# First products of W_o's gradient between the last sums of the recurrence's backward pass, and LayerNorm loads behind three chunks of rows

## The chip, the core and the metric

The kernel runs on one core of one Trainium2 chip. Its time is the device time of one execution in microseconds (us); the median of several executions counts. Five engines run beside each other: TensorE (PE) multiplies, VectorE (DVE) and ScalarE (ACT) empty accumulators and do elementwise work, GpSimd (POOL) copies and issues DMAs, SyncE (SP) issues DMAs. Each runs its own instructions in order and waits on semaphores for the others.

## What is computed

One transformer layer, forward and backward: the output and the gradients of all eleven inputs that have one. A recurrent attention block with 32 heads of 128 goes through 64 segments of 32 tokens, with 8 memory rows handed from segment to segment; a gated MLP follows; both stand behind a LayerNorm that is scaled and shifted by rows made from `c` and `w_mod`. What bears on the change:

```python
for s in range(n_seg):                                   # 64 segments, in order
    h = jnp.concatenate([mem, xs], axis=1)               # 8 memory rows + 32 tokens = 40 rows
    q, k, v = (einsum('btd,dhe->bhte', h, W) for W in (Wq, Wk, Wv))
    ...
    o = jnp.einsum('bhqk,bhke->bhqe', p, v)
    o = jnp.einsum('bhte,hed->btd', o, Wo)
    mem = o[:, :M, :]
_out, _vjp = jax.vjp(_f, A_x, A_mem0, A_Wq, A_Wk, A_Wv, A_Wo, B_w_gate, B_w_up, B_w_down, c, w_mod)
```

W_o's gradient is, for each head, the product of two row matrices over all 64 x 40 rows: the attention output before W_o, and the gradient after W_o. The gradients of Wq, Wk and Wv are such products too.

## The kernel before

The program is one long list of instructions in phases; the two at whose border the change lies are `phase4` and `phase5`. A scheduler puts the instructions of each engine in order by what it holds to be ready, unless `pin` forbids it: `pin(i0, engines)` chains all instructions traced since `i0` on each engine in the order of the program text, and `pin_behind` puts all of a stretch behind one instruction.

**Phase 4, the recurrence backward.** A loop over the 64 segments, last one first, pinned on all engines. Each segment ends in a 512-column sum `dh_ps` of 64 narrow products, a second sum of the query part (`dhq_ps`, folded to `dh_ft`), and a row store to `DHA`, whose second half (turn by TensorE, copy by VectorE, store by GpSimd) is put off in a list `later` and taken out by `pop_later`. The 8 last rows of each segment (the *tail*) are gathered for four segments at a time; class `TailRows` multiplies them by the three weights in 96 narrow products `dh_tps` in seven pieces (16, 24, 8, 8, 16, 8, 16), one piece per call of `chunk`. `split` then writes the sum as two bf16 halves, hi by ScalarE and lo by VectorE (L312, L313), into tile `dS`; 8 products fold them (`dh_b_ft`, L323), VectorE casts (L331), TensorE turns (`dh_b_tp`, L335), VectorE copies (L337), and GpSimd stores to `DHB` (L341). The tail of group 1 (segments 4 to 7) is worked off within the last segments. That of group 0 is collected in the last segment, so `finish` (L2225 on) runs all of it behind the loop: split of group 1, all seven pieces of group 0, split of group 0, then everything in `later`. Its sum lives in the single bank of pool `psb`, which group 1's sum holds until its split. The loop's other accumulators are six banks of pool `psp`, tag `p`.

**Phase 5, weight gradients and the first LayerNorm backward.** 36 chunks: nine for W_o, then nine each for Wq, Wk, Wv. A chunk has up to four heads, its rows are loaded into `rows5` (three buffers; 20 positions x up to 512 columns on 128 partitions), and each head of a W_o chunk is one bank `gps5o` with 20 products of 512 columns (L2121). Pool `psG` has four banks. `load_rows(i + 2)` is issued at chunk `i`; the first three chunks' rows go on SP's queue alone, by `rows_in` (L1931), later ones half on ScalarE's. Chunk 0 is prepared during the last segment: `p5_first` loads the gradient rows (`dyrows`, L1918) and 12 of chunk 0's 20 positions (`rows_a`) into the place of `WoT`, which is free by then, and `p5_second` (L1939) the gradient's memory rows. So 48 of chunk 0's 80 products read only these (the profile writes `WoT`); the other 32 wait for the rest of the chunk's rows. SP's loads are pinned among themselves from `load_rows(0)` to the loads of chunk 5; LayerNorm's are not in that chain.

The LayerNorm part goes through 16 tiles of 128 rows (`ln_tile`): loads of `x0`, of the gradient rows `dhb` in eight pieces from `DHA` and `DHB` (L362, L363) and of `dx1` (L1981), VectorE statistics (L1990), two products into a sum (`acc_ps`, L1999 and L2002), and a store. `ln_load(0)` stands at chunk 5 in the text, and `ca1_bc` (L369) is loaded at the top of the phase.

Of the kernel before, what the change touches and what calls it, by code (L numbers as in the profile page):

```python
# [7 lines left out]
BF16 = mybir.dt.bfloat16  # L8
F32 = mybir.dt.float32
# [3 lines left out]
PSUM = bass.MemoryType.PSUM  # L13
# [27 lines left out]
class K:  # L41
# [1502 lines left out]
    def phase4(self):  # L1544
        nc, tc, cfg, io = self.nc, self.tc, self.cfg, self.io
        D, DC, H, E, L, M, T, G, NS = cfg.D, cfg.DC, cfg.H, cfg.E, cfg.L, cfg.M, cfg.T, cfg.G, cfg.NS
# [5 lines left out]
        with self.p4_ctx as ctx:  # L1552
# [3 lines left out]
            pt = ctx.enter_context(tc.tile_pool(name="p4pt", bufs=1, reuse_waits="tile"))  # L1556
            rxp = ctx.enter_context(tc.tile_pool(name="p4rx", bufs=3, reuse_waits="tile"))
            sb2 = ctx.enter_context(tc.tile_pool(name="p4s2", bufs=2, reuse_waits="tile"))
            psp = ctx.enter_context(tc.tile_pool(name="p4ps", bufs=6, space=PSUM, reuse_waits="tile"))
            psb = ctx.enter_context(tc.tile_pool(name="p4psb", bufs=1, space=PSUM, reuse_waits="tile"))  # L1560
            NP = 3
            PG = 4
# [133 lines left out]
            i0 = len(self.traced())  # L1696
# [14 lines left out]
            i0 = len(self.traced())  # L1711
            for s in reversed(range(NS)):
# [175 lines left out]
                g = s // 4  # L1888
# [10 lines left out]
                then = None  # L1899
                if s == 0:  # L1900
                    def then(rb):
                        nc.sync.dma_start(io["out_2"].rearrange("o m (c x) -> (o m c) x", c=DC), rb[0:M * DC, :])

                self.store_rows(psp, sb2, ft, self.DHA[s], "dh", "p", then)
                if s4 == 0:
                    tail.begin(s, [WvT, WkT, WqT])
            store_rows_x(0)
            self.pin(i0)
            tail.finish()

    def p5_first(self):

# [8 lines left out]
    def rows_in(self, dst, dram, hl, g0, ng, a, b, o, qs):  # L1921
# [3 lines left out]
        for k, runs in enumerate((((0, Q, 32 * hl), (Q, Q + T2, 32 * hl + M)),  # L1925
                                  ((0, Q, 32 * hl + Q), (Q, c, 32 * hl + M + T2), (c, Q + T2, 96 + 8 * hl)))):
            to = dst.rearrange("(s k) t x -> k s t x", k=2)[k]
            for t0, t1, r in runs:
                lo, hi = max(a, t0), min(b, t1)
                if lo < hi:  # L1930
                    qs[k].dma_start(to[:, lo - o:hi - o, 0:ng * E],  # L1931
                                    dram[:, r + lo - t0:r + hi - t0, g0:g0 + ng, :].rearrange("s t g e -> s t (g e)"))

    def p5_second(self):

        nc, cfg, M, NS = self.nc, self.cfg, self.cfg.M, self.cfg.NS
        Q = M // 2
        for k in range(2):
            nc.sync.dma_start(self.dyrows[:, 0:Q, :].rearrange("(s k) t d -> k s t d", k=2)[k],  # L1939
                              self.DHA[1:NS + 1, Q * k:Q * k + Q, :])  # L1940

    def phase5(self):
# [7 lines left out]
        assert KR <= 128  # L1950
        with ExitStack() as ctx:
            ctx.enter_context(self.wo_ctx)
            rp = ctx.enter_context(tc.tile_pool(name="p5g_r", bufs=1, side="right", reuse_waits="tile"))
            hrows = rp.tile([128, NTP, D], BF16, name="hrows")
            lp = ctx.enter_context(tc.tile_pool(name="p5g_l", bufs=3, reuse_waits="tile"))
# [2 lines left out]
            sb1 = ctx.enter_context(tc.tile_pool(name="p5a_s1", bufs=1, reuse_waits="tile"))  # L1958
            sb2 = ctx.enter_context(tc.tile_pool(name="p5a_s2", bufs=2, reuse_waits="tile"))
            psAcc = ctx.enter_context(tc.tile_pool(name="p5a_psAcc", bufs=1, space=PSUM, reuse_waits="tile"))  # L1960
            ca1_bc = self.mod_bc(wp, 1, "ca1_bc", plus_one=True)
            sel = wp.tile([128, 2, 128], BF16, name="sel5")
            nc.vector.memset(sel[:], 0.0)
            for i in range(2):
# [87 lines left out]
            if not getattr(cfg, "skip_wgrad", False):  # L2052
                Q, T2, A = M // 2, T // 2, self.p5_ahead
                op_ = ctx.enter_context(tc.tile_pool(name="p5g_o", bufs=3, reuse_waits="tile"))
                psG = ctx.enter_context(tc.tile_pool(name="p5g_ps", bufs=4, space=PSUM, reuse_waits="tile"))
                kk = [0]

                def next_eng():
                    kk[0] += 1
                    return "act" if kk[0] % 2 == 0 else "dve"  # L2060

                def load_h(k):
                    if k == 0:
                        nc.sync.dma_start(hrows[:, Q:NTP, :], self.H1ROWS[:, :].rearrange("(p t) d -> p t d", t=T2))
                        return
                    for i in range(2):
                        nc.sync.dma_start(hrows[:, 0:Q, :].rearrange("(s k) t d -> k s t d", k=2)[i],
                                          self.AOA[0:NS, Q * i:Q * i + Q, :])

                chunks = [(hl, g0, min(4, (H - hl + 2) // 3 - g0)) for hl in range(3) for g0 in (0, 4, 8)]  # L2070
                todo = [(x, kind, outw, ch) for (x, kind, outw) in ((self.OSR, "o", io["out_6"]), (self.DQR, "qkv", io["out_3"]),
                                                                  (self.DKR, "qkv", io["out_4"]), (self.DVR, "qkv", io["out_5"]))
                        for ch in chunks]
                loaded = {}

                def load_rows(i):
                    if i >= len(todo) or i in loaded:
                        return
                    x, _, _, (hl, g0, ng) = todo[i]
                    t = loaded[i] = lp.tile([128, NTP, 4 * E], BF16, name="rows5")  # L2080
                    self.rows_in(t[:, :, :], x, hl, g0, ng, 0, NTP - A if i == 0 else NTP, 0,
                                 (nc.sync, nc.sync if i < 3 else nc.scalar))

                i0 = len(self.traced())
                load_rows(0)
                load_rows(1)
                load_rows(2)
                n_ln = len(todo) - 6
                for i, (_, kind, outw, (hl, g0, ng)) in enumerate(todo):
                    load_rows(i + 2)  # L2090
                    if 4 <= i <= 5:
                        load_h(i - 4)
                    if i == 5:
                        self.pin(i0, [mybir.EngineType.SP])
                    rows = loaded.pop(i)
                    if i == 5:
                        ln_load(0)
                    while ln_done[0] * (n_ln - 5) < (i - 5) * NT and ln_done[0] < NT:
                        ln_step()
                    if i >= n_ln:  # L2100
                        mod_grads(i - n_ln)
                    h0 = 3 * g0 + hl
                    if kind == "qkv":
                        for c in range(DC):
                            ps = psG.tile([128, 4 * E], F32, name="gps5", tag="g")
                            for tp_ in range(NTP):
                                nc.tensor.matmul(ps[:, 0:ng * E], lhsT=hrows[:, tp_, c * 128:(c + 1) * 128],  # L2107
                                                 rhs=rows[:, tp_, 0:ng * E], start=(tp_ == 0), stop=(tp_ == NTP - 1))
                            ot = op_.tile([128, 4 * E], BF16, name="ot5")
                            self.evac(next_eng(), ot[:, 0:ng * E], ps[:, 0:ng * E])  # L2110
                            nc.gpsimd.dma_start(outw[c * 128:(c + 1) * 128, h0:h0 + 3 * (ng - 1) + 1:3, :],  # L2111
                                                ot[:, 0:ng * E].rearrange("p (h e) -> p h e", e=E))
                    else:
                        pss = [psG.tile([128, D], F32, name="gps5o", tag="g") for _ in range(ng)]
                        order = list(range(NTP - A, NTP)) + list(range(Q, NTP - A)) + list(range(Q))
                        parts = (order[0:6], order[6:A], order[A:NTP - Q], order[NTP - Q:]) if i == 0 else (order,)
                        for part in parts:
                            for gg in range(ng):
                                for tp_ in part:
                                    src = (self.rows_a, tp_ - NTP + A) if i == 0 and tp_ >= NTP - A else (rows, tp_)  # L2120
                                    nc.tensor.matmul(pss[gg][:], lhsT=src[0][:, src[1], gg * E:(gg + 1) * E], rhs=dyrows[:, tp_, :],  # L2121
                                                     start=(tp_ == order[0]), stop=(tp_ == order[-1]))
                        for gg, ps in enumerate(pss):
                            ot = op_.tile([128, D], BF16, name="ot5o")
                            self.evac(next_eng(), ot[:], ps[:])
                            nc.gpsimd.dma_start(outw[h0 + 3 * gg], ot[:])
    def run_pipeline(self, n, stages, deepest_first=False, after=lambda it: None):
        ns = len(stages)
        states = {}
        for it in range(n + ns - 1):  # L2130
            for k in (reversed(range(ns)) if deepest_first else range(ns)):
                j = it - k
                if 0 <= j < n:
                    states[j] = stages[0](j) if k == 0 else stages[k](j, states[j])
                    if k == ns - 1:
                        states.pop(j, None)
            after(it)
# [26 lines left out]
class TailRows:  # L2164
# [57 lines left out]
        self.k.later.append(summed)  # L2222
        return True

    def finish(self):  # L2225
        self.split()
        while self.pieces:
            self.chunk()
        self.split()
        while self.k.later:  # L2230
            self.k.pop_later()

# [84 lines left out]
```

## Time and profile before

| what | value |
|---|---|
| median of 3 runs | 3039.75 us (3037.28 to 3044.77) |
| the profiled execution's own time | 3037.14 us |
| its span, first to last instruction | 3035.4 us |
| TensorE busy, mean granted clock | 2958.5 us (97%), 0.995 |
| last product of the loop's last segment starts | 2458.33 us |
| first product of chunk 0 (data of the last segment's loads) | 2468.22 us |
| first product of chunk 0 that needs rows loaded in phase 5 | 2479.81 us |
| first product of chunk 1 | 2487.53 us |
| first and last LayerNorm products (`acc_ps`) | 2565.3 us, 2926.3 us |

All moments are microseconds from the span's start. A line of the timeline gives start, duration, engine, source line, operation and tile, a count of like instructions merged, and in brackets the idle time of the engine before it with what ended it. `PE` durations include the way through the array; like products start closer together than they last. `SPq` is SP as an issuer of DMAs. `WoT<-DAROWS` and `WoT<-OSR` are the early loads for chunk 0, `rows<-OSR` those of phase 5.

### The profile page before, as it was taken

To read this page: it belongs to the slowest core of one execution; us is meant where nothing else is said; L and a number is where in the kernel's file an instruction comes from. 1 tells how busy PE (TensorE), PEld (TensorE's weight loads), DVE (VectorE), ACT (ScalarE), POOL (GpSimd) and SP (SyncE) were. 2 spreads that over 40 slices of the span, in tenths; PEclk is the share of its full clock that TensorE was granted. 3 is DMA by queue.
4 is the path that set the end of the run, shared out by engine and by line. 5 is a ranking of instruction groups with operands and counts; after the bars stand their busy time and mean duration, and the time that the engine had idled before them with its cause. 6 is when DMAs were issued, how large, how long until landed. Compare 5 with 4: busy or idle time off the path is not lost.

```text
span 3035.4 us, 106027 instructions
## 1 busy us (share of the span) xinstructions
PE 2958.5 (97%) x43975; PEld 1852.1 (61%) x44049; DVE 1605.5 (53%) x3746; ACT 1290.0 (42%) x3185; POOL 1219.8 (40%) x2642
## 2 busy tenths in 40 slices
PE   6999999999998999999999999999999999999999
PEld 3666666666665544446577777777777754445454
DVE  5566656656655788723455555555555532222221
ACT  2555555555554533312355555555555521101111
POOL 2555555555545222211244444444444422333322
PEclk9999999999999999999999999999999999999999
DMA  9888888888889899988699999999999997666574
GB/s 305 220 223 204 212 224 213 208 218 214 212 210 275 208 229 227 246 258 262 188 245 249 248 245 247 248 248 246 246 248 247 246 287 258 224 194 217 175 242 148
DMA packets 837350, 703.15 MB, mean 232 GB/s; under 512 B 537634, under 2 KB 709826, under 8 KB 835972
## 3 DMA queue, kind: packets, MB, share of 16 engines
q1 hardware_dynamic: 709764, 484.85, 63.9%
q0 software_dynamic: 54512, 148.63, 15.5%
q10 hardware_dynamic: 72592, 62.89, 6.7%
q8 instruction: 346, 5.67, 0.8%
q14 instruction: 136, 1.11, 0.1%
HBM read 295.09 MB, written 276.35 MB: 188 GB/s over the span
## 4 chain that ended last, share of the span: by engine, by line
PE 89%; DMA 4%; issue 3%; DVE 2%; ACT 1%; POOL 1%; SPq 0%; another core or an unknown queue 0%; DVEq 0%; POOLq 0%; ACTq 0%
PE pass_ps L255 14%; PE gps L2107 11%; PE dh_ps L215 8%; PE g_ps L1768 6%; PE pass_ps L658 5%; PE gps5o L2121 4%; PE dhq_ps L223 4%; PE at_ps L223 4%; PE gps L1444 3%; PE mm L1286 3%; PE dh_tps L215 3%; PE turn_ps L828 2%; PE dp_ps L1745 2%; PE tps L1676 2%; PE mm L1261 1%
## 5 line engine op out<-in xcount | busy, mean ns | idle before, releaser
L2107 PE MATMUL gps<-rows,hrows 128*128 128x512 bf16 (+2 forms) x2124 | 415.6, 355 | 1.9
L2107 PEld LDWEIGHTS <-hrows 128*128 128x128 bf16 x2160 | 211.2, 98 | 204.6
L61 ACT ACTIVATE ot<-gps 128x512 bf16<-128x512 f32 (+3 forms) x75 | 41.3, 551 | 371.8 <-PE gps L2107 211.6
L1813 POOL COPY dOst<-RAd 96x512 bf16<-96x512 bf16 x128 | 75.5, 614 | 302.2 <-DVE RAd L63 302.2
L63 DVE CAST ot<-gps 128x512 bf16<-128x512 f32 (+3 forms) x76 | 48.2, 634 | 273.9 <-PE gps L2107 186.8
L658 PE MATMUL pass_ps<-Wv,hT 128*32 128x512 bf16 (+2 forms) x2304 | 188.2, 357 | 0.0
L2111 POOL DMA_DIRECT2D out_dram<-ot x108 | 81.6, 755 | 260.6 <-DVE ot L63 135.8
L255 PEld LDWEIGHTS <-hT 128*32 128x32 bf16 x4096 | 125.1, 97 | 95.3 <-DMA Wq<-in_A_Wq_dram 5.9
L1034 POOL TENSOR_TENSOR Pst<-Pst,rden 120x1408 bf16<-120x1408 bf16 x63 | 159.9, 2538 | 50.7 <-issue 27.2
L61 ACT ACTIVATE dVT<-g_ps 128x480 bf16<-128x480 f32 (+1 forms) x192 | 104.6, 545 | 95.6 <-PE g_ps L1768 95.1
L63 DVE CAST Vst<-pass_ps 96x512 bf16<-96x512 f32 x128 | 87.3, 682 | 106.5 <-ACT RBv L61 99.8
L215 PE MATMUL dh_ps<-WvT,dVT 128*32 128x512 bf16 x2048 | 134.5, 383 | 0.2
L255 PE MATMUL pass_ps<-Wq,hT 128*32 128x512 bf16 x2048 | 125.6, 383 | 5.8 <-DMA Wq<-in_A_Wq_dram 5.8
L2121 PE MATMUL gps5o<-WoT,rows 128*128 128x512 bf16 x580 | 127.8, 379 | 2.4 <-DMA rows<-OSR 1.7
L223 PE MATMUL at_ps<-Wo,OT 128*32 128x256 bf16 x4096 | 124.6, 274 | 3.0 <-DMA Wo<-in_A_Wo_dram 2.6
L658 PE MATMUL pass_ps<-Wv,hb 128*32 128x512 bf16 (+2 forms) x636 | 127.3, 346 | 0.0
L255 PE MATMUL pass_ps<-Wk,hT 128*32 128x512 bf16 x2048 | 124.1, 379 | 1.8 <-POOL hT L547 1.1
L793 POOL DMA_DIRECT2D Vst<-RBv x192 | 99.6, 524 | 59.7 <-ACT ET L840 38.2
L255 PE MATMUL pass_ps<-WoT,dyT 128*32 128x256 bf16 (+1 forms) x3072 | 122.4, 308 | 0.9 <-ACT dyT L1887 0.9
L223 PE MATMUL dhq_ps<-WqT,dQT 128*32 128x256 bf16 x4096 | 122.9, 273 | 0.0
L215 PE MATMUL dh_ps<-WkT,dKT 128*32 128x512 bf16 x2048 | 122.3, 380 | 0.0
L223 PEld LDWEIGHTS <-dQT 128*32 128x32 bf16 x4096 | 109.6, 97 | 15.9
(457 smaller groups left out, 6976.1 us busy)
## 6 DMA issues: line engine op xcount, KB each, us to landing
OSR<-Ost SPq DMA_DIRECT2D x64, 352.0 KB
OT<-OT SPq DMA_DIRECT2D x64, 352.0 KB
VT<-VTr SPq DMA_DIRECT2D x64, 352.0 KB
PS<-Pst SPq DMA_DIRECT2D x64, 352.0 KB
OT_l<-OT SPq DMA_DIRECT2D x64, 352.0 KB
Pst_l<-PS SPq DMA_DIRECT2D x64, 352.0 KB
VT_l<-VT SPq DMA_DIRECT2D x64, 352.0 KB
DVR<-rows_x POOLq DMA_DIRECT2D x64, 352.0 KB, 5.9
```

The costliest lines, as they stand in the source:

```text
L61: return nc.scalar.activation(out, in_, AF.Copy)
L63: return nc.vector.tensor_copy(out, in_)
L215: self.nc.tensor.matmul(ps[32 * j:32 * j + 32, :], lhsT=lhsT, rhs=w, start=(n < 4), stop=(n >= total - 4), tile_position=(0, 32 * j))
L223: nc.tensor.matmul(ps[32 * j:32 * j + 32, :], lhsT=x[k], rhs=w[k][:, 256 * d:256 * d + 256], start=(n == 0), stop=(n == total - 1), tile_p ...
L255: self.nc.tensor.matmul(ps[32 * j:32 * j + 32, :], lhsT=lhs(c), rhs=rhs, start=(c == 0), stop=(c == DC - 1), tile_position=(0, 32 * j))
L658: nc.tensor.matmul(ps[32 * j:32 * j + 32, o * E:(o + n) * E], lhsT=lhsT, rhs=wc[:, 3 * a + hl:3 * (a + n - 1) + hl + 1:3, :], start=(c == ...
L793: nc.gpsimd.dma_start(Vst[96 + 8 * j:104 + 8 * j, :], rb[32 * j + o:32 * j + o + 8, :])
L1034: nc.gpsimd.tensor_tensor(Pst[0:120, :, :], Pst[0:120, :, :], rden[:, :].unsqueeze(2).to_broadcast([120, G, 128]), op=ALU.mult)
L1286: nc.tensor.matmul(hp[:], lhsT=xT[:, fc, :], rhs=wT[:, fc, :], start=(n == 0), stop=(n == 2 * FC - 1))
L1768: nc.tensor.matmul(ps[:, j, 0:w], lhsT=lh[:, g * GW:(g + 1) * GW], rhs=rh[:, g * GW:g * GW + w], start=True, stop=True)
L2107: nc.tensor.matmul(ps[:, 0:ng * E], lhsT=hrows[:, tp_, c * 128:(c + 1) * 128], rhs=rows[:, tp_, 0:ng * E], start=(tp_ == 0), stop=(tp_ == ...
L2121: nc.tensor.matmul(pss[gg][:], lhsT=src[0][:, src[1], gg * E:(gg + 1) * E], rhs=dyrows[:, tp_, :], start=(tp_ == order[0]), stop=(tp_ == o ...
```

## The change

- `psp`, the six banks of the recurrence, stays open into phase 5 and takes the place of `psG`. The tail's last sum (`dh_tps` of group 0) takes a bank of `psp` instead of the one of `psb`.
- `finish` takes one entry out of `later` behind each piece of the tail. Behind the last piece the split goes to a tile of `rxp` instead of `dS`; then three groups of 16 products of chunk 0 (positions 0 to 3, 4 to 7 and 8 to 11 of its order, four heads each) are issued, with one entry of `later` taken out behind each.
- TensorE's order in `finish` is pinned, behind the loop.
- In phase 5, `ca1_bc` and `ln_load(0)` are issued at chunk 1, in SP's chain behind the rows of chunks 0, 1 and 2; every later DMA of SP is put behind the chain's end.
- The store of `out_2` goes from SP's queue to GpSimd's.

```diff
@@ phase4
+            self.ps_ctx = ExitStack()
+            psp = self.psp = self.ps_ctx.enter_context(tc.tile_pool(name="p4ps", bufs=6, space=PSUM, reuse_waits="tile"))
...
                     def then(rb):
-                        nc.sync.dma_start(io["out_2"].rearrange("o m (c x) -> (o m c) x", c=DC), rb[0:M * DC, :])
+                        nc.gpsimd.dma_start(io["out_2"].rearrange("o m (c x) -> (o m c) x", c=DC), rb[0:M * DC, :])
...
             store_rows_x(0)
-            self.pin(i0)
-            tail.finish()
+            last, i0 = self.pin(i0), len(self.traced())
+            tail.psb, tail.ptag = psp, "p"
+            tail.finish([lambda k=k: self.p5_products(range(4 * k, 4 * k + 4)) for k in range(3)],
+                        rxp.tile([128, G, 128], BF16, name="rows_x")[:].rearrange("p g x -> p (g x)"))
+            self.pin(i0, [mybir.EngineType.PE])
+            self.pin_behind(i0, last, [mybir.EngineType.PE])
...
+    def p5_chunk0(self):
+
+        D, NTP, Q, A = self.cfg.D, self.cfg.L // 2, self.cfg.M // 2, self.p5_ahead
+        self.p5_order = list(range(NTP - A, NTP)) + list(range(Q, NTP - A)) + list(range(Q))
+        self.p5_ps = [self.psp.tile([128, D], F32, name="gps5o", tag="p") for _ in range(4)]
+
+    def p5_products(self, ks, rows=None):
+
+        if ks[0] == 0:
+            self.p5_chunk0()
+        E, NTP, A, order = self.cfg.E, self.cfg.L // 2, self.p5_ahead, self.p5_order
+        for gg, ps in enumerate(self.p5_ps):
+            for k in ks:
+                t = order[k]
+                src = (rows, t) if t < NTP - A else (self.rows_a, t - NTP + A)
+                self.nc.tensor.matmul(ps[:], lhsT=src[0][:, src[1], gg * E:(gg + 1) * E], rhs=self.dyrows[:, t, :],
+                                      start=(k == 0), stop=(k == NTP - 1))
@@ phase5
-            ca1_bc = self.mod_bc(wp, 1, "ca1_bc", plus_one=True)
+            ca1_bc = wp.tile([128, D], F32, name="ca1_bc")
...
-                psG = ctx.enter_context(tc.tile_pool(name="p5g_ps", bufs=4, space=PSUM, reuse_waits="tile"))
...
                 for i, (_, kind, outw, (hl, g0, ng)) in enumerate(todo):
+                    if i == 1:
+                        self.mod_bc(wp, 1, "ca1_bc", plus_one=True, t=ca1_bc)
+                        ln_load(0)
                     load_rows(i + 2)
                     if 4 <= i <= 5:
                         load_h(i - 4)
-                    if i == 5:
-                        self.pin(i0, [mybir.EngineType.SP])
                     rows = loaded.pop(i)
                     if i == 5:
-                        ln_load(0)
+                        last, i1 = self.pin(i0, [mybir.EngineType.SP]), len(self.traced())
...
+                        if i == 0:
+                            pss = self.p5_ps
+                            self.p5_products(range(A, NTP - Q), rows)
+                            self.p5_products(range(NTP - Q, NTP), rows)
...
+                self.pin_behind(i1, last, [mybir.EngineType.SP])
@@ TailRows
-    def finish(self):
+    def finish(self, between=(), home=None):
         self.split()
         while self.pieces:
             self.chunk()
+            if between:
+                self.k.pop_later()
+        if between:
+            self.home = home
         self.split()
+        for f in between:
+            f()
+            self.k.pop_later()
         while self.k.later:
             self.k.pop_later()
```

More of the change, by code (lines that the diff above doesn't have):

```diff
@@ L1558, in phase4 @@
             sb2 = ctx.enter_context(tc.tile_pool(name="p4s2", bufs=2, reuse_waits="tile"))
-            psp = ctx.enter_context(tc.tile_pool(name="p4ps", bufs=6, space=PSUM, reuse_waits="tile"))
+            self.ps_ctx = ExitStack()
+            psp = self.psp = self.ps_ctx.enter_context(tc.tile_pool(name="p4ps", bufs=6, space=PSUM, reuse_waits="tile"))
             psb = ctx.enter_context(tc.tile_pool(name="p4psb", bufs=1, space=PSUM, reuse_waits="tile"))
@@ L1952, in phase5 @@
             ctx.enter_context(self.wo_ctx)
+            ctx.enter_context(self.ps_ctx)
+            psG = self.psp
             rp = ctx.enter_context(tc.tile_pool(name="p5g_r", bufs=1, side="right", reuse_waits="tile"))
@@ L2104, in phase5 @@
                         for c in range(DC):
-                            ps = psG.tile([128, 4 * E], F32, name="gps5", tag="g")
+                            ps = psG.tile([128, 4 * E], F32, name="gps5", tag="p")
                             for tp_ in range(NTP):
@@ L2113, in phase5 @@
                     else:
[L2114 to L2117, printed above, removed]
+                        if i == 0:
+                            pss = self.p5_ps
+                            self.p5_products(range(A, NTP - Q), rows)
+                            self.p5_products(range(NTP - Q, NTP), rows)
+                        else:
+                            pss = [psG.tile([128, D], F32, name="gps5o", tag="p") for _ in range(ng)]
                             for gg in range(ng):
[L2119 to L2122, printed above, removed]
+                                for n, t in enumerate(self.p5_order):
+                                    nc.tensor.matmul(pss[gg][:], lhsT=rows[:, t, gg * E:(gg + 1) * E], rhs=dyrows[:, t, :],
+                                                     start=(n == 0), stop=(n == NTP - 1))
                         for gg, ps in enumerate(pss):
```

## The prediction

> **What bounds the kernel.** I read the page first (busy time, then the chain that ended last):
>
> ```profile
> PE 2958.5 (97%) x43975; PEld 1852.1 (61%) x44049; DVE 1605.5 (53%) x3746; ACT 1290.0 (42%) x3185; POOL 1219.8 (40%) x2642
> PE 89%; DMA 4%; issue 3%; DVE 2%; ACT 1%; POOL 1%; SPq 0%; another core or an unknown queue 0%; DVEq 0%; POOLq 0%; ACTq 0%
> ```
>
> TensorE is the bound: a change gains only by closing holes between its products. Next come TensorE's waits. From 2490 us to the end the view is empty. In the stretch 2458 to 2490 us, which the change rebuilds, it says (total, times, longest):
>
> ```profile
> PE gps5o L2121 <- DMA rows<-OSR: 1.7, 2, 1.1
> PE dh_b_ft L323 <- ACT dS L312: 0.7, 1, 0.7
> PE dh_b_tp L335 <- DVE dh_b_rb L337: 0.5, 1, 0.5
> PE dh_tp L335 <- DVE dh_tb L331: 0.5, 1, 0.5
> PE dh_b_tp L335 <- DVE dh_b_tb L331: 0.4, 1, 0.4
> PE dh_tps L215 <- DVE dh_rb L337: 0.4, 1, 0.4
> PE dh_b_ft L323 <- DVE dS L313: 0.4, 1, 0.4
> ```
>
> Eight holes. TensorE's timeline places them and gives the pace of the products:
>
> ```profile
> 2458.33 0.27 PE L240 MATMUL dh_ft<-foldsel,dh_lo 128*128 128x32 bf16 x4
> 2459.76 1.91 PE L215 MATMUL dh_tps<-WvT,dh_tail 128*32 128x512 bf16 x32 [0.40 <-DVE dh_rb L337]
> 2461.49 1.91 PE L215 MATMUL dh_tps<-WkT,dh_tail 128*32 128x512 bf16 x32
> ...
> 2468.22 10.52 PE L2121 MATMUL gps5o<-WoT 128*128 128x512 bf16 x47
> 2479.81 7.07 PE L2121 MATMUL gps5o<-WoT,rows 128*128 128x512 bf16 x31 [1.07 <-DMA rows<-OSR]
> 2487.53 12.70 PE L2121 MATMUL gps5o<-WoT,rows 128*128 128x512 bf16 x57 [0.66 <-DMA rows<-OSR]
> ```
>
> Last SP's own timeline: between the last segment's transposes and the rows of chunk 0 stand LayerNorm's loads, and one of them waits for the tail's store:
>
> ```profile
> 2461.01 2.90 SPq L1776 DMA_TRANSPOSE rows_x<-dQT  x1
> 2464.01 0.53 SPq L1902 DMA_DIRECT2D out_dram<-dh_rb  x1
> ...
> 2472.47 0.26 SPq L363 DMA_DIRECT2D dhb<-DHB  x1
> 2472.83 0.34 SPq L369 DMA_DIRECT2D ca_bc<-MODROW  x1
> 2473.23 33.02 SPq L1931 DMA_DIRECT2D rows<-OSR  x18
> ```
>
> **The sum.** From 2458.33 to the first product of chunk 1 at 2487.53 TensorE does a fixed lot of work, the same before and after. By start-to-start pace: 32 tail products take 1.73 us (2459.76 to 2461.49), 0.054 each, so 96 take 5.19. A chunk product takes 0.219 (49 in 10.74 us in the chain), so 80 take 17.54. Two folds of 8 (0.30 each in the chain) 0.60, three turns of 0.06 0.18, the four products at the start 0.15. Together 23.66 us of 29.20. The difference, 5.5 us, is what the holes cost; their idle columns add up to 4.71 (0.54, 0.40, 0.70, 0.36, 0.44, 0.54, 1.07, 0.66), because each stop also loses the overlap of a product's way through the array (it lasts 0.379 and starts every 0.219).
>
> **Tail and folds, part by part.** (1) The first piece no longer needs the bank that group 1 holds until its split ends at 2459.62; it can start at 2458.48, and the turn `dh_tp`, whose cast ends at 2459.08, comes behind 16 products (0.87 us): both first stops go. (2) The fold of group 1 then comes behind 24 more products, at 2460.7; its halves are there since 2459.62. (3) Its turn needs the cast, about 0.5 us from fold to turn (2458.60 to 2459.13 in the last segment), and only 8 products (0.43) cover that. A stop of 0.1 to 0.3 is new; I take 0.2. (4) 48 products more bring 2464.2. The split of group 0 (0.60 and 0.69 us, L312 and L313) lies beside 16 chunk products (3.5 us), the cast (0.44) beside the next 16, the copy and store beside the last 16. (5) Accumulators: chunk 0 holds four of six banks, the tail's sum one until about 2465.8. If the third head is given that one, it wants it at 2466.0, so 0 to 0.3; I take 0, for other banks are long empty.
>
> **Early data.** The products now start at 2464.2, not 2468.2. What they read was issued from 2445.82 to 2451.5 (3.5 MB); 2450 to 2460 ran at 403 and 379 GB/s, and the transposes behind on the same queue show from 2461 on. So it lies there by about 2463. Price 0 to 4.0 us (the old start proves only 2468.2); I take 0.
>
> **Rows.** SP is free at 2464.0 and goes straight to chunk 0's rows, 9.2 us earlier. The 48 products end at 2475.1, the next 16 need rows. Before, the first rows were there 6.6 us after the first issue (2473.23 to 2479.81) and chunk 1's 14.3 us after it (2487.49). Now the transposes fill the DMA engines until 2466 (100% in 2464 to 2466), and the stores of `DKR` and `DQR` (0.35 MB each) come in between, 2 us at 340 GB/s, while `ca1_bc` (0.26 MB, 0.8 us) stands behind. Chunk 0: 2464.0 + 6.6 + 2 to 3 = 2472.6 to 2473.6, before 2475.1. Chunk 1: 2464.0 + 14.3 + 1.2 to 3.2 = 2479.5 to 2481.5; wanted at 2482.2. Margin 0.7 us and more: chunk 0's two stops go, the second only just. Chunk 2 waits for the `DQR` store (issued 2468.07, such stores land in 3.0 to 5.0 us) and is wanted at 2499.7; its 2 MB take 6 us.
>
> The Trainium skill ("DMA: Bandwidth & Descriptors", Anatomy of one DMA) gives a DMA about 2.0 us plus its bytes at 436 GB/s. By it the 3.93 MB before would have taken 11.0 us; the trace shows 14.3, so the trace's value is used. By the rule the margin of chunk 1 would be over 3 us and its rival below would lose most of its chance.
>
> **Moved without price.** The `out_2` store: 0.53 us off SP, 0.54 us onto GpSimd, which then idles 4.9 us to 2465.51. LayerNorm tile 0 loads some 12 us later (SP reaches it at about 2476), and GpSimd's store of group 0's `DHB` row goes from 2468.6 to about 2472.3, landing 3.9 us on; behind these loads on SP stands only chunk 3, whose buffer is free at 2482 and wanted at 2513. Tile 0's first product is at 2565.3. Tile 1 loads behind chunk 5's loads, at about 2550, for products at 2578 (2583.1 before): 28 us of cover, and if it were gone each us would stall TensorE. Six banks instead of four only relax the evacuations. VectorE (53% busy) and ScalarE (42%) have room.
>
> Sum: 5.5 - 0.2 = 5.3 us. The profiled execution, 3037.14 us (1.74 around its span of 3035.4), becomes 3031.8. The median of the runs shown is 2.6 above that execution, and the forecast goes by the median: 3039.75 - 5.3 = **3034.4**. A measurement of this kernel can tell some 0.3%, 9.1 us, from no change: no hole that could bring that is in this stretch.
>
> **Rivals.**
> *Chunk 1's rows come late.* SP's issue of them meets the stores or waits for earlier loads (SP waits for its own `rows` loads at 2486 to 2500 before). By 1 to 3 us: 3035.5 to 3037.5. For it: the thin margin. 15%.
> *It does not do what it says for the rows*: a buffer of chunks 0 or 1 lies over tiles still read, and SP's first issue stays near 2472. The two DMA stops, shifted, take back most: chunk 1 at 2472 + 14.3 = 2486.3, gain 1.2, 3038.5. Against it: the transposes read these tiles until 2467.6 at most. 9%.
> *Slower: VectorE waits for LayerNorm.* Only TensorE is pinned in the tail. Before, VectorE took `x0`'s statistics at 2468.67, right behind the tail's copies. If the scheduler sets them ahead of group 0's cast, TensorE's turn, now pinned in front of the last 16 early products at 2471.7, waits for `x0`. That load now stands behind 5.6 MB of rows; with stores about 6.6 MB from 2466 on, at 335 GB/s, and 1.8 us to report (before, chunk 0's bytes had moved by 2478 and TensorE went on at 2479.81): 2487.5; statistics 0.69 and cast 0.44 make 2488.7. A hole of 17 us. It also costs clock:
>
> ```profile
> 1495.28 0.56 PE L1768 MATMUL g_ps<-Pst_l,dOst 128*128 128x120 bf16 x4 [5.40 <-DMA dOst<-RBd]
> 1496.00:1498.00 2.00, 2.00 (x23) 2.00 (x21) 0.00 (x0) 0.75 (x2) 0.83 (x5) 0.50 0.01 4
> ```
>
> Behind a hole of 5.40 us the granted clock (third from the right) is 0.50, and 1.00 again from 1502: some 2.7 us lost. Net 17.0 + 2.7 - 5.3 = 14.4 slower, 3054. It decides as soon as the cast is over 2472. For it: VectorE's operations were drawn ahead already (`dc_t` at 2463.45). Against it: by any reckoning `x0` is ready long after the cast's input. 9%.
>
> The Trainium skill ("TensorE: Matmul & The Clock Gate", Part 1: The HAM clock gate) has the clock halved after about 3.4 us of idleness; a hole of 3.30 us at 1316.6 already left 0.55 behind it here. No hole of the forecast is near either.
>
> **How the numbers follow.** Forecast 61%, late rows 15%, rows as before 9%, VectorE 9%, other (a lucky median, an order better than I see) 6%. The own range of the forecast is 3031 to 3037 (the runs before spread over 7.5 us, the early data up to 4). With both middle rivals, their spread and the low end: 3029.5 to 3042; the VectorE case and half of the last are left out. Faster by over 0.3%: 7%, a median below 3030.6; slower by over 0.3%: 10%; within: 83%.
>
> **What would show it.** TensorE's waits from 2458 to 2485: one of about 0.2 at `dh_b_tp`, none for `rows<-OSR`, none for `dS`; first chunk product near 2464.2, chunk 1 near 2482.2; SP's first `rows<-OSR` near 2464. A wait of chunk 1's first product shows rival one, a late first issue rival two, a hole at the second `dh_b_tp` rival three. Any wait of TensorE behind 2500, at `acc_ps` above all, would show LayerNorm's loads too late, which this sum holds for covered.

## The result, and the profile after

The changed kernel takes 3033.84 us in the median of 22 runs (3029.84 to 3047.09) against 3039.78 for the kernel before in 22 runs beside it; the ratio is 0.9984, 95% interval 0.9976 to 0.9992, so 2.4 to 7.3 us less. The forecast was 3034.4, 5.3 less.

The page's first lines of the changed kernel. TensorE's share has risen by one point. It also leads the chain that ended last as before, with 86% (89% before), and "issue" has 5% there (3%); that shift was not taken apart.

```profile
span 3033.1 us, 106112 instructions
PE 2963.8 (98%) x44049; PEld 1853.1 (61%) x44049; DVE 1605.2 (53%) x3746; ACT 1288.1 (42%) x3185; POOL 1215.5 (40%) x2643
```

TensorE's timeline of the rebuilt stretch in the changed kernel (start, duration, what, count; a bracket would show idle time):

```profile
2461.21 0.27 PE L240 MATMUL dh_ft<-foldsel,dh_lo 128*128 128x32 bf16 x4
2461.41 1.05 PE L215 MATMUL dh_tps<-WvT,dh_tail 128*32 128x512 bf16 x16
...
2464.26 0.61 PE L215 MATMUL dh_tps<-WkT,dh_tail 128*32 128x512 bf16 x8
2464.87 0.23 PE L335 MATMUL dh_b_tp<-ident,dh_b_tb 128*128 128x128 bf16 x1
...
2467.73 3.63 PE L1954 MATMUL gps5o<-WoT 128*128 128x512 bf16 x16
2471.20 0.36 PE L323 MATMUL dh_b_ft<-foldsel,rows_x 128*128 128x32 bf16 x8
...
2478.36 7.07 PE L1954 MATMUL gps5o<-WoT,rows 128*128 128x512 bf16 x32
2485.27 15.06 PE L2147 MATMUL gps5o<-WoT,rows 128*128 128x512 bf16 x69
```

No line has a bracket, and the view of TensorE's waits is empty from 2458 us to the end: all eight stops are gone. From the second `dh_ft` products to chunk 1's first product, **the stretch** from here on, it is 2485.27 - 2461.21 = 24.06 us, against 29.20 before: 5.14 us less. This execution came to the stretch 2.88 us later than the one before (2461.21 against 2458.33), in work that the change does not touch. So the spans differ by 2.3 us only (5.14 - 2.88), and single executions are compared by the stretch.

SP's timeline of the changed kernel:

```profile
2464.32 2.87 SPq L1777 DMA_TRANSPOSE rows_x<-dQT  x1
2467.30 19.28 SPq L1936 DMA_DIRECT2D rows<-OSR  x14
2486.62 0.70 SPq L369 DMA_DIRECT2D ca_bc<-MODROW  x1
2495.36 0.34 SPq L2002 DMA_DIRECT2D x<-in_A_x_dram  x1
```

The rows do follow the transposes at once. But their 14 loads take 19 us to issue, and SP's waits say why: the first load of chunk 1, the fifth in all, is held until 2475.85, until a store of `DQR` has landed.

```profile
SPq L1936 <- DMA DQR<-rows_x: 5.3, 1, 5.3
```

### The profile page after: what moved, and what is told of

Read it like the earlier page. It is cut to its first block, busy times and chain, and to the rows that moved or that the text cites. A ratio compares the mean times of both kernels' runs of the same rounds, so it can differ in the third digit from the quotient of the medians.

```text
span 3033.1 us, 106112 instructions
## 1 busy us (share of the span) xinstructions
PE 2963.8 (98%) x44049; PEld 1853.1 (61%) x44049; DVE 1605.2 (53%) x3746; ACT 1288.1 (42%) x3185; POOL 1215.5 (40%) x2643
## 4 chain that ended last, share of the span: by engine, by line
PE 86%; issue 5%; DMA 4%; DVE 2%; POOL 1%; ACT 1%; SPq 0%; ACTq 0%; POOLq 0%; DVEq 0%
PE pass_ps L255 14%; PE gps L2132 9%; PE dh_ps L215 8%; PE g_ps L1769 6%; PE pass_ps L658 5%; PE gps5o L2147 4%; PE dhq_ps L223 4%; PE at_ps L223 4%; PE gps L1444 3%; PE mm L1286 3%; PE dh_tps L215 3%; PE turn_ps L828 2%; PE dp_ps L1746 2%; PE tps L1677 2%; PE mm L1261 1%
## 5 line engine op out<-in xcount | busy, mean ns | idle before, releaser
L2147 PE MATMUL gps5o<-WoT,rows 128*128 128x512 bf16 x560 | 121.4, 379 | 0.0
```

The costliest lines, as they stand in the source:

```text
L2147: nc.tensor.matmul(pss[gg][:], lhsT=rows[:, t, gg * E:(gg + 1) * E], rhs=dyrows[:, t, :], start=(n == 0), stop=(n == NTP - 1))
```

## The experiments

The theory: the change is worth the sum of its stops, those for rows through the loads' part and those of the tail through the rest, and the two need each other. The rivals are in the texts on record. Every kernel is read by its stretch, from one profiled execution each; where several runs were timed, the ratio to the kernel before stands beside it. The two kernels that were profiled twice agree with themselves within 0.2 us.

| kernel | stretch, us | expected by the theory |
|---|---|---|
| before; once more | 29.20; 29.36 | 29.2 or about 30.7 |
| changed; once more | 24.06; 24.05 | 24.0 to 24.6 |
| loads_only | 28.85 (27.2 at full clock) | 27.2 |
| products_only | 33.35 | 32 to 33 |
| tail_old_bank | 25.29 | 25.3 |
| products_behind | 26.23 | 26.2 to 26.4 |
| hrows_early | 30.60 | 26.7 to 27.7 |
| four_buffers | 25.19 | 24.0 to 24.2 |
| small_loads_first | 25.19 | 24.0 to 24.2 |
| ln_behind_two | 24.05 | 24.0 to 24.2 |
| second_late | 24.05 | 24.0 to 24.1 |
| second_late_small | 24.18 | 24.0 to 24.1 (A), 24.1 to 25.2 (B) |

**The loads' part alone (loads_only).**

```diff
+                    if i == 1:
+                        self.mod_bc(wp, 1, "ca1_bc", plus_one=True, t=ca1_bc)
+                        ln_load(0)
                     load_rows(i + 2)
...
+                self.pin_behind(i1, last, [mybir.EngineType.SP])
```

> The kernel before with the loads' part alone: ca1_bc and LayerNorm tile 0 behind the rows of three chunks, later SP loads behind that chain; tail, products and banks as before. Read in the stretch from the last segment's second dh_ft products to chunk 1's first product (29.20 us before, 24.06 with the whole change). My theory: SP issues the first rows right behind the transposes, some 9 us earlier, so TensorE's two stops for rows (1.07 and 0.66, and 0.16 of lost overlap each) go and the six stops of the tail stay: stretch 27.2, time 2.0 us less. Rival (the rows were late for their buffers, not for LayerNorm): stretch 29.2, time the same.

Measured: ratio 0.9995 (0.9984 to 1.0005), not told from no change. Both stops for rows are gone and the tail's six are left, as expected, but from the first of the 48 early products to the next one behind them it takes 12.05 us (2470.93 to 2482.98). In the kernel before, at the pace of 0.216 us of these products, it would be 10.36 (the 10.52 of its line hold the last product's way through the array too):

```profile
2470.93 12.21 PE L2122 MATMUL gps5o<-WoT 128*128 128x512 bf16 x47
```

The table by stretches (each engine's busy time, then TensorE's granted clock, third from the right) shows the reason:

```profile
2472.00:2474.00 2.00, 2.00 (x6) 0.76 (x5) 0.00 (x0) 0.00 (x0) 1.09 (x3) 0.50 1.05 345
2474.00:2476.00 2.00, 2.00 (x8) 0.79 (x7) 0.00 (x0) 0.00 (x0) 0.00 (x0) 0.76 0.56 218
```

The clock fell to half behind the tail, which cost 1.7 us; from 2476 on it is 1.00 again. With 32 products behind 2482.98 chunk 1 starts near 2489.9, so the stretch is 28.85, and 27.2 without the clock's loss: the loads' part would be worth 2.0 us at full clock. This is a corrected figure of one execution; the runs' ratio does not show it.

**All but the loads' part (products_only).** In the changed kernel:

```diff
-            ca1_bc = wp.tile([128, D], F32, name="ca1_bc")
+            ca1_bc = self.mod_bc(wp, 1, "ca1_bc", plus_one=True)
...
-                    if i == 1:
-                        self.mod_bc(wp, 1, "ca1_bc", plus_one=True, t=ca1_bc)
-                        ln_load(0)
...
+                    if i == 5:
+                        self.pin(i0, [mybir.EngineType.SP])
                     rows = loaded.pop(i)
                     if i == 5:
-                        last, i1 = self.pin(i0, [mybir.EngineType.SP]), len(self.traced())
+                        ln_load(0)
...
-                self.pin_behind(i1, last, [mybir.EngineType.SP])
```

> The whole change without its loads' part: tail, products between the sums and shared banks as changed, ca1_bc and LayerNorm's loads as before. My theory: the rows still stand behind LayerNorm's loads on SP, and these wait for group 0's DHB store, which the interleaving makes about 3.7 us later; so the first rows go out near 2477 on before's clock, TensorE runs dry behind its 48 early products for some 8 us, and chunk 1 starts 3 to 4 us later than before: stretch 32 to 33, slower by 3 to 4 us. Rival (the tail's six stops carry the gain by themselves): stretch 25.5 to 26, faster by 3.5 us. Between them: the scheduler sends the rows ahead of the waiting load, stretch 29, no change.

Measured: ratio 1.0014 (1.0005 to 1.0023), slower; stretch 33.35, 4.15 more than before. TensorE's timeline, SP's, and the clock behind the stop:

```profile
2470.00 3.62 PE L1954 MATMUL gps5o<-WoT 128*128 128x512 bf16 x15
2480.50 9.31 PE L1954 MATMUL gps5o<-WoT,rows 128*128 128x512 bf16 x32 [6.89 <-DMA rows<-OSR]
2489.64 15.70 PE L2146 MATMUL gps5o<-WoT,rows 128*128 128x512 bf16 x70
```

```profile
2470.51 0.43 SPq L2048 DMA_DIRECT2D wmod<-in_w_mod_dram  x1
2471.04 0.37 SPq L369 DMA_DIRECT2D ca_bc<-MODROW  x1
2471.46 36.89 SPq L1936 DMA_DIRECT2D rows<-OSR  x18
```

```profile
2482.00:2484.00 2.00, 2.00 (x6) 0.72 (x5) 0.00 (x0) 0.00 (x0) 0.00 (x0) 0.50 1.11 349
```

The tail's stops are gone, and the time they held comes back as one stop of 6.89 us for rows, behind which the clock is halved. The 4.15 us add up: the first rows are used 24.21 us behind the `dh_ft` products instead of 21.48 (2.73 more), 32 products take 9.14 us instead of 6.91 (2.23 more), and the stop of before at chunk 1, 0.8 from start to start, is gone. The size was as expected; the wait that I had named was not. In the kernel before SP does wait for a store to `DHB`:

```profile
SPq L363 <- DMA DHB<-dh_b_rb: 2.3, 1, 2.3
```

Here it does not: four loads of `DHB` run through from 2467.60, the other four are set behind the rows at 2508. The first rows go out 15.17 us behind the `dh_ft` products, as before (14.90); a `w_mod` load of 0.77 MB that now stands just ahead of them would take 2.3 us at 340 GB/s and fits the rest, which was not tried by itself.

**The tail's bank (tail_old_bank) and the products' place (products_behind).**

```diff
-            tail.psb, tail.ptag = psp, "p"
```

> The whole change, but group 0's tail sum in the old single bank, which group 1's sum holds until its split has ended. My theory: the first piece waits for VectorE's lo half as before, 1.2 to 1.3 us, and nothing gives that back: stretch 25.3. Rival (chunk 1's rows come only just in time in the changed kernel, so TensorE's lead there is worth nothing): stretch 24.1 to 24.4.

```diff
         self.split()
+        while self.k.later:
+            self.k.pop_later()
         for f in between:
             f()
-            self.k.pop_later()
-        while self.k.later:
-            self.k.pop_later()
```

> The whole change, but chunk 0's 48 early products behind the last fold and turn instead of between them. My theory: split (0.60 and 0.69), fold, cast (0.44) and turn of group 0 stand bare again: TensorE stops about 2.2 us, stretch 26.2 to 26.4. Rival (these stops are hidden in the wait for rows anyway): stretch 24.1 to 24.5.

Measured: 25.29 (1.23 lost) and 26.23 (2.17 lost). Stops come back at the same places of the work. In tail_old_bank it is one at the tail's first piece, in place of the two of before around it, and VectorE's lo half ends it; in products_behind there are three at group 0's folds and turn:

```profile
2469.71 1.05 PE L215 MATMUL dh_tps<-WvT,dh_tail 128*32 128x512 bf16 x16 [1.17 <-DVE dS L313]
```

```profile
2467.82 0.27 PE L323 MATMUL dh_b_ft<-foldsel,rows_x 128*128 128x32 bf16 x4 [0.75 <-ACT rows_x L312]
2468.55 0.27 PE L323 MATMUL dh_b_ft<-foldsel,rows_x 128*128 128x32 bf16 x4 [0.46 <-DVE rows_x L313]
2469.35 0.23 PE L335 MATMUL dh_b_tp<-ident,dh_b_tb 128*128 128x128 bf16 x1 [0.54 <-DVE dh_b_tb L331]
```

With the loads' 2.0 the parts make 2.0 + 1.23 + 2.17 = 5.4 us; the whole is 5.14. So they add up within 0.3 us, but they are not measured in one way: the loads' part was put into the kernel before by itself and corrected for the clock, the other two were taken out of the changed kernel. Taken out of the changed kernel in the same way, the loads' part costs 9.3 us (33.35 against 24.06): without it the rest is a loss.

**How much cover chunk 1's rows have.** Cover is the time from the rows being there to TensorE wanting them.

```diff
                 load_rows(0)
+                load_h(0)
                 load_rows(1)
```

> The whole change, with the 2 MB load of hrows (needed only from chunk 9 on) taken from chunk 4's place on SP to the place between chunk 0's and chunk 1's rows. In the changed kernel SP sends chunk 1's first load only at 2475.85, when the DQR store has landed, and TensorE wants it at 2485.27 without a stop; the DMA engines stand about 2.3 us idle in 2474 to 2478. My theory: chunk 1's rows come within about 1 us of being late, so the 2 MB (5.9 us at 340 GB/s, 2.3 of them in the idle time) make chunk 1 start 2.6 to 3.6 us later: stretch 26.7 to 27.7 against 24.06, one stop of TensorE at chunk 1's first product. Rival (the rows have the cover of 1 to 5 us that the prediction worked out, or more): stretch 24.1 to 25.

```diff
-            lp = ctx.enter_context(tc.tile_pool(name="p5g_l", bufs=3, reuse_waits="tile"))
+            lp = ctx.enter_context(tc.tile_pool(name="p5g_l", bufs=4, reuse_waits="tile"))
```

> The whole change with four buffers for rows instead of three, so that another place may fall to chunk 1. Nothing waits for rows in the changed kernel, so both theories expect the same time in the stretch, 24.0 to 24.2. What is asked is SP's fifth load of rows: if the wait until 2475.85 is that of a buffer lying over the rows which the DQR store reads, another layout may move it to another load; if it stays, at 8.5 us behind the first issue, it comes from elsewhere.

The `out_2` store back on SP, and:

```diff
+                self.mod_bc(wp, 1, "ca1_bc", plus_one=True, t=ca1_bc)
                 load_rows(0)
```

> The whole change, with the out_2 store back on SP and ca1_bc ahead of the first rows, as in the kernel before. My theory: the first rows go out 0.9 to 1.0 us later, behind which 48 early products lie; chunk 1's rows wait for a store and not for SP, so the stretch stays at 24.0 to 24.2: these two moves are worth nothing, only LayerNorm's loads are. Rival (every us of SP ahead of the rows counts): stretch 24.5 to 25.0.

All three missed, on the same side. TensorE's chunk 1 and SP's wait for the fifth load, in hrows_early, four_buffers and small_loads_first:

```profile
2499.87 20.43 PE L2149 MATMUL gps5o<-WoT,rows 128*128 128x512 bf16 x83 [6.38 <-DMA rows<-OSR]
SPq L1936 <- DMA DQR<-rows_x: 10.4, 1, 10.4
```

```profile
2488.06 32.10 PE L2147 MATMUL gps5o<-WoT,rows 128*128 128x512 bf16 x148 [0.97 <-DMA rows<-OSR]
SPq L1936 <- DMA DHB<-dh_b_rb: 7.2, 1, 7.2
```

```profile
2490.47 29.73 PE L2147 MATMUL gps5o<-WoT,rows 128*128 128x512 bf16 x137 [0.97 <-DMA rows<-OSR]
SPq L1936 <- DMA DKR<-rows_x: 3.0, 1, 3.0
SPq L1936 <- DMA DQR<-rows_x: 2.9, 1, 2.9
```

In each the fifth load still waits for a store, in four_buffers for another one than before. That its buffer takes over the tiles which the store reads is my reading; no view shows the places. It goes out 16.25 us behind the `dh_ft` products in four_buffers (2479.12) and 16.33 in small_loads_first (2481.61), 14.64 in the changed kernel. From there chunk 1's rows need 8.94 and 8.86 us until TensorE goes on; the changed kernel has 9.42. So its cover is some 0.5 us (0.85 by second_late_small below, which needs 8.57). In small_loads_first GpSimd issues the `DQR` store as early as in the changed kernel (10.29 us behind the `dh_ft` products against 10.41), but it holds the fifth load 1.7 us longer; with `ca1_bc` on the DMA engines at that time this fits, and it was not taken apart. So these two small moves are worth about 1 us in this pair of executions, which my theory had denied. In hrows_early the 2 MB delay the store as well as the rows, so it cost 6.5 us and not 3.

**Behind two chunks (ln_behind_two).** `ca1_bc` and `ln_load(0)` between `load_rows(1)` and `load_rows(2)`:

> The whole change, with ca1_bc and LayerNorm tile 0 behind the rows of two chunks instead of three. My theory: chunk 2's rows are wanted 17.5 us after chunk 1's start, so ten small loads ahead of them, one of which waits for the DHB store, cost nothing: stretch 24.0 to 24.2 and no stop at chunk 2. Rival (SP's issue of chunk 2 is already late, since it waits for earlier loads until 2486): a stop of 1 to 5 us at chunk 2's first product.

Measured: 24.05, no stop at chunk 2 or later. The third chunk's place ahead of LayerNorm is worth nothing in this execution.

**An earlier store (second_late, second_late_small).** `p5_second` moved behind the last segment's transposes, in the changed kernel and in small_loads_first:

> The whole change, with the gradient's memory rows (p5_second, 0.25 MB, whose load waits on SP 5.3 us for a store of the segment before) issued behind the last segment's two transposes instead of ahead of them. Chunk 1's fifth load of rows waits for the DQR store, that for the dQT transpose, and that stands behind this waiting load on SP. Theory A (SP's order sets it): transposes, DQR store and chunk 1's first load come 3 to 4 us earlier against the last dh_ft products (fifth load at 10.6 to 11.6 us behind them, 14.64 in the changed kernel). Theory B (the DMA engines, full until 2461 with the early loads, set it): at most 1 us earlier. In both the stretch stays at 24.0 to 24.1 and the time is that of the changed kernel, since no stop is left there to be taken away; slower by 1 us and more only if the memory rows come late.

> small_loads_first (a stop of 0.97 us at chunk 1, fifth load 16.33 us behind the dh_ft products) with the same move. Theory A: fifth load 3 to 4 us earlier, the stop gone, stretch 24.0 to 24.1. Theory B: stop of 0 to 0.97 left, stretch 24.1 to 25.2.

Measured: stretch 24.05, ratio to before 0.999 (0.9979 to 1.0002). GpSimd issues the `DQR` store 8.98 us behind the `dh_ft` products instead of 10.41, but it lands later after its issue, and the fifth load goes out at 14.67, as before the move: the measure of theory B (at most 1 us earlier) holds, and theory A's 3 to 4 us are out. That the DMA engines set it was not tried by itself. In second_late_small the load comes 0.7 us earlier (15.61) and the stop of 0.97 is gone but for 0.12 (24.18 against 24.06), too short for a bracket.

**Both kernels once more.**

> The changed kernel once more, unaltered. Chunk 1's rows take 8.9 us from the fifth load where TensorE waited for them, and had 9.42 us in the profile at hand: a margin of 0.5. Theory: the stretch is 24.0 to 24.6, with a stop of 0 to 0.5 us at chunk 1; a stop of 1 us and more would show that the margin is often negative and the change often worth less than 5.1 us.

> The kernel before once more, unaltered. In loads_only, which keeps the six short stops of the tail, the granted clock fell to 0.50 from about 2471.6 to 2475 behind them, and 48 products took 12.05 us instead of 10.52; in the profile of before the same stops left the clock at 1.00. Theory (stops of 0.4 to 0.7 us within some 5 us can let the clock drop, depending on where they fall): the stretch is either 29.2 again or about 30.7 with a clock of 0.5 behind the tail. Rival (the drop belongs to loads_only alone): 29.2, clock 1.00. A second 29.2 would leave it open.

The changed kernel: 24.05, no stop. The kernel before: its two stops for rows are now one of 1.84 us, the stretch is 29.36 (products that need rows from 2486.61, the first of chunk 1 at 2493.73), the clock 1.00 all along. So the drop of loads_only did not come again, and how often the tail's stops bring it stays open.

## Why the prediction was right, point by point

- **The bound and the sum.** Right in kind: 5.3 us forecast, 5.14 gained, and the idle columns alone (4.71) would have been too little. That it is so close is in part luck, for two sizes were off and nearly cancel. A chunk product starts every 0.216 us and not every 0.219 (32 take 6.91 us, from 2478.36 to 2485.27); the chain's 49 products in 10.74 us must be 50, since some records are missing. That is 0.25 us less work for 80. In return some 0.1 us goes at most borders between unlike products, which the sum left out: the 48 tail products from 2465.03 take 2.70 us to 2467.73, not 2.59, and the turn at 2464.87 holds 0.16 us, not 0.06.
- **Tail and folds.** Right by both undoings. The new stop of 0.2 us at `dh_b_tp` is there without a bracket: 8 tail products from 2464.26 would end at 2464.69, and the turn starts at 2464.87, 0.18 later.
- **Accumulators and early data.** No stop at the third head, nor at the first early product (2467.73, which is 2464.85 on before's clock, 0.6 later than forecast). The early data lay there by then; how much sooner is not shown.
- **Rows.** The step failed inside, and the forecast held by 0.5 to 0.85 us of cover. I had put the wait for the `DQR` store at chunk 2's buffer; it is at chunk 1's. Chunk 1's first load came 14.64 us behind the `dh_ft` products, 3.1 us earlier than before (2476.07) and not the some 9 us by which the first rows moved. From the first issue (2467.30, 6.09 us behind the `dh_ft` products) the rows took some 17.1 to 17.5 us, which lies in the 14.3 + 1.2 to 3.2 that I had added up. That is luck: I had added the bytes of two stores, and what came in between was a wait of 5.3 us for one of them. The rule that the prediction takes from the Trainium skill ("DMA: Bandwidth & Descriptors", Anatomy of one DMA) is given there for DMAs on GpSimd's path. The loads here are SP's, and the margin of over 3 us by that rule did not show.
- **Moved without price.** The prices were nothing, as forecast, but not the moment: SP reached tile 0's `x0` at 2495.36 (2492.5 on before's clock), not at 2476, since the rows' loads ahead wait for each other. TensorE's first LayerNorm product is past 2562 and it does not wait anywhere behind 2500.
- **Rivals.** Late rows did not happen, yet are one small move away (0.97 us twice). The second, rows as before, was half true for chunk 1: its first load was held back by a store, and only chunk 0's rows moved as far as forecast. The third (VectorE ahead of the cast) did not happen: the statistics stand at 2499.41, behind chunk 0. It was not tried by itself; the price of its clock part can be read from products_only: 2.23 us behind a stop of 6.89, where I had put 2.7, read behind a hole of 5.40.
- **The clock.** The Trainium skill ("TensorE: Matmul & The Clock Gate", Part 1: The HAM clock gate) has the clock halved after about 3.4 us of idleness. The stop of 6.89 us agrees: the clock is 0.50 behind it. In loads_only no stop was over 0.70 us and the clock fell all the same; TensorE was busy for 1.67 of the 3.60 us before. The measurement decides: the clock can fall without one long stop. It did so in one of three executions with these stops, and what set it off is not shown.

## What to carry to other kernels

When stops of the bounding engine are closed ahead of a transfer, the transfer must move too: one part alone turned 3.4 us of gain (1.23 and 2.17) into 4.2 of loss here. Count a stop from start to start, count products by a stretch with no record missing, and ask for each load not only where it stands in its queue but which store still reads the buffer that it fills. A gain that rests on a cover of less than a microsecond should be tested by moving something small.

## What the hardware showed that was not expected

The granted clock fell to 0.50 for about 3.4 us behind six stops of 0.36 to 0.70 us in one execution (loads_only) and stayed at 1.00 behind the same stops in two (before and its repetition), with nearly the same busy time of TensorE (1.67, 1.68 and 1.81 us of the last 3.60). It cost 1.7 us, nearly as much as the loads' part brings. And moving a waiting load out of the way made a store issue 1.4 us earlier without making it land earlier.
